# The forms of seven experts' W1 made while the routing runs, and new orders at both ends of the middle stage

## The chip, the cores and the metric

The kernel runs on one core of one Trainium2 chip. The metric is the time that one execution takes on the device, in microseconds (us); the kernel before was timed in three runs and the median counts. The engines are named as in the profile: PE is TensorE's matrix products and PEld its weight loads, DVE is VectorE, ACT is ScalarE, POOL is GpSimd, SP is SyncE. SPq and POOLq are the instructions by which an engine issues transfers (DMA). Each engine works through its own instructions in order, and a transfer is issued only when its engine has come to it.

## The reference

Attention with a polynomial sketch gives x: 4352 rows (4 batches of 1088) by 128 columns. Eight experts then work on every row, and a Sinkhorn normalization of the gate gives the weights P with which they are summed. All of it is float32.

```python
q_p, k_p = (phi(q), phi(k))                  # 64 sketch features per row
kv = np.einsum('bhsf,bhsd->bhfd', k_p, v)
z = np.sum(k_p, axis=2)
num = np.einsum('bhsf,bhfd->bhsd', q_p, kv)
den = np.einsum('bhsf,bhf->bhs', q_p, z)[..., None] + 1e-06
x = ...                                      # (4352, 128) from num / den
P = np.exp(logits - logits.max())            # logits = x @ w_gate, (4352, 8)
for _ in range(8):
    P /= P.sum(1, keepdims=True) + 1e-09
    P /= P.sum(0, keepdims=True) + 1e-09
    P *= N / E
for e in range(E):                           # w1[e]: 128 x 1024, w2[e]: 1024 x 128
    h = np.maximum(x @ w1[e], 0.0)
    out += P[:, e:e + 1] * (h @ w2[e])
```

## The kernel before

**Items and blocks.** The experts' work is cut into items: one expert with one group of columns of the transposed x (`xT`). An item has four blocks, each a quarter of the 1024 hidden units. Items that come early use x without the weights and keep their outputs (`kept`), which are weighted later; all others use x already multiplied by P. The expert products are computed by fast matrix products: sums of blocks of the operands are made first, so that fewer products are needed, and sums of the results afterwards. Which sums of W1 an item reads does not hang on x, so they can be made early: `forms_ahead` (line 256) makes two arrays in device memory for an expert, `wl` and `wf`. Expert 0 needs none, since all its items lie outside the middle stage.

**How the forms of one expert are made.** `forms_ahead(e, area)` returns nine jobs: `loads` (two copies of raw W1 into `wl`, three loads into the working area), `turn_all`, `turn_low`, `turn_lowest`, `turn_across` (four ScalarE instructions that copy with the sign turned, line 282; two of them also issue an addition), `keep_low`, `last_sum`, `keep_two`, `keep_rest`. Additions are transfers issued by POOL that add to their target (line 276); copies and stores are transfers issued by SP (line 279). The working area is 3 x 512 elements on each of 128 partitions.

**Three stages.** First comes the attention of the four batches, then the routing; both are generators whose `yield n` calls `fill(n)`, which lets the plain stage of the experts' work take steps beside them. The plain stage is `steps()`: first products of 128 rows in line 1113, relus in line 1117, second products in line 1546. `passed[0]` counts its steps, and `aside` holds jobs by step number. In `routing()` the forms of experts 1 to 5 (`AHEAD = 5`) are put into `aside`, the first from 7 steps after the routing's start and each next one 6 steps later, with the nine jobs at 0, 5, 6, 7, 11, 12, 15, 16 and 20 steps. Their areas are the tile `kp` and the attention's buffers `phs` and `rb`, one for each of four experts in turn. The routing ends with four transfers from `qT` to `pT` (line 696), the weights by expert; weighted items read rows of `pT` into `px`.

**The list at the end of the plain stage.** `TAIL` (line 1560) holds what is done beside the last two plain items, by step: it weights the first item of the middle stage (`weigh_half`, `copy_half`, `join_halves`), loads its raw W2 (`raw_second`) and its W1 forms, and weights the two halves of the second item. `first_second_forms` loads `wf` in two halves into `y` tiles; `first_weights`, when it comes after it, then loads `wl` alone, and when it comes first, both `wl` into a `w1` tile and `wf` into a `w2` tile. `w1` and `w2` tiles are also those of the plain stage.

**The middle stage.** `middle()` writes out by hand the order of 68 blocks (34 items). Each job has a time, and jobs are issued in the order of their times; the times set nothing but this order. A block has 28 first products of 64 x 64 in line 1279 (seven forms for each of two pairs of tiles), evacuations of them by ACT (lines 1308, 1310, 1314) and DVE (line 1319), sums on DVE (`SUMS`, line 1181) and 40 second products in line 1546. The usual times repeat every `PERIOD`:

```python
at_ = own[n] if 0 <= n < len(own) and own[n] is not None else n * PERIOD + usual
```

For the first four blocks the times come from a table, `SEAM`. Beside the blocks stand the loads of later items: `first_weights` (`w<-wl`, `w<-wf`), `raw_second` (`ws<-in_moe_w_dram`), `fetch_weights` (`px<-pT`). An expert's W2 forms are made from raw W2 by DVE (line 238) and ACT (line 241) the first time it is used, and stored with `keep_second` (line 251). In the second item's start `SEAM` has its two copies on ACT and four joins on POOL (line 842, `x2a` and `x2b`). The forms of W1 of experts 6 and 7 are also made here, in a tile `forms`, with the same nine jobs as in the routing (`forms_beside`, line 1557), expert 6 from block 1 on and expert 7 from block 5 on.

**The end.** After the last block of the middle stage, three unweighted blocks (`EARLY = 3`) take their first products (`step_of_two`) while the last sums go on. A last group follows, and the rest of the outputs are stored.

## Time and profile before

| What | Value |
|---|---|
| Median of 3 runs | 895.38 us (895.25 to 897.02) |
| Profiled execution, its own time | 898.83 us |
| Span of its instructions | 897.0 us |
| Granted TensorE clock, mean | 0.997 |
| TensorE busy, 0 to 175 us (attention, routing) | 171.2 us |
| TensorE busy, 175 to 235 us (end of plain stage, head of middle stage) | 58.6 of 60 us |
| TensorE busy, 235 to 327 us | 85.6 of 92 us |
| TensorE busy, 327 to 816 us | 489.0 of 489 us |
| TensorE busy, 816 to 897 us | 75.5 of 81 us |
| Device memory read and written | 125.7 MB and 25.1 MB |

The span runs from the first instruction to the last. A row of the profile names a line of the kernel, an engine, an operation and the tiles as output<-inputs, with partitions x elements and the count; a bracket at the end says how long the engine stood idle ahead of it, and what it waited for. A row of the table by stage has the window, then its length, the busy time of PE, PEld, DVE, ACT and POOL with the number of instructions, the granted clock, the share of the DMA engines that was busy, and GB/s. In the chain of waits the first figure is the time at which a step begins and the second its length. A row of transfers has the count, the size of each and the time from issue to landing.

### The profile page before, as it was taken

Reading aid. Unit: us, or ns where it says so; the run is one execution under the profiler, and the core shown is the slowest. Engines: PE = TensorE matmul, PEld = TensorE weight load, DVE = VectorE, ACT = ScalarE, POOL = GpSimd, SP = SyncE. Lnnn points to the kernel's source line nnn. Section 1 sums busy time; section 2 is a strip of 40 time slices with the busy share of each in tenths; the row PEclk is TensorE's granted clock in tenths of the full one; section 3 lists DMA queues with packets and bytes.
Section 4 is the critical chain, followed back from the end, with each engine's and each line's share of the span. In section 5 each row is a group of like instructions: output and inputs, shape, how many; then the busy total and the mean of one; then the engine's idle time right before and its main releaser. Section 6 shows DMA issues by size and latency. Waiting matters only on the chain.

```text
span 897.0 us, 28696 instructions
## 1 busy us (share of the span) xinstructions
PE 880.0 (98%) x11790; PEld 640.2 (71%) x11790; DVE 792.7 (88%) x1628; ACT 572.1 (64%) x1312; POOL 176.5 (20%) x244
## 2 busy tenths in 40 slices
PE   8999999999998989999999999999999999999997
PEld 6777644454776768887778878888778777766665
DVE  7678788888999979999999999899998999997865
ACT  3455477668776647676676766766766766755543
POOL 3121123112222212212212211231122122200000
PEclk9999999999999999999999999999999999999999
DMA  9996359687899777976787676787668776764340
GB/s 253 300 269 229 106 105 223 151 205 197 215 269 260 177 231 207 249 219 164 209 234 199 176 221 158 226 223 213 194 158 226 213 223 179 213 190 89 90 112 13
DMA packets 97459, 174.67 MB, mean 195 GB/s; under 512 B 29216, under 2 KB 68976, under 8 KB 92480
## 3 DMA queue, kind: packets, MB, share of 16 engines
q1 hardware_dynamic: 74832, 139.67, 49.7%
q0 software_dynamic: 21264, 33.00, 21.3%
q8 instruction: 93, 1.52, 0.7%
q10 hardware_dynamic: 1232, 0.16, 0.1%
q14 instruction: 38, 0.31, 0.1%
HBM read 125.70 MB, written 25.08 MB: 168 GB/s over the span
## 4 chain that ended last, share of the span: by engine, by line
PE 92%; DMA 4%; DVE 2%; ACT 1%; issue 0%; SPq 0%; POOL 0%; DVEq 0%; ACTq 0%
PE s L1546 41%; PE a L1279 36%; PE a L1113 12%; DMA kx<-in_k_dram 1%; PE a L419 1%; DMA w<-wf 1%; PE a L534 1%; DMA forms<-in_moe_w_dram 1%; DMA v<-in_v_dram 1%; DMA w<-wl 1%; DVE hb L1132 0%; PE a L386 0%; ACT hb L1314 0%; PE a L498 0%; DVE hb L1181 0%
## 5 line engine op out<-in xcount | busy, mean ns | idle before, releaser
L1279 PE MATMUL a<-xe,w 64*64 64x384 f32 x2164 | 419.7, 485 | 0.0
L1546 PE MATMUL s<-hb,ws 64*64 64x256 f32 (+4 forms) x2962 | 382.7, 384 | 1.8 <-DVE hb L1132 0.9
L1546 PE MATMUL s<-hx,ws 64*64 64x256 f32 (+1 forms) x2894 | 353.1, 378 | 0.0
L1279 PE MATMUL a<-de,w 64*64 64x384 f32 x1600 | 305.9, 483 | 6.1 <-DMA w<-wf 3.9
L1546 PEld LDWEIGHTS s<-hb,ws 64*64 64x64 f32 (+1 forms) x2962 | 207.0, 133 | 72.9 <-issue 23.1
L1546 PEld LDWEIGHTS s<-hx,ws 64*64 64x64 f32 (+1 forms) x2894 | 201.3, 134 | 54.1 <-issue 7.9
L1181 DVE TENSOR_TENSOR hb<-hb 128x512 f32<-128x512 f32 (+1 forms) x340 | 187.7, 577 | 2.3 <-ACT hb L1314 2.1
L1279 PEld LDWEIGHTS a<-xe,w 64*64 64x64 f32 x2164 | 147.3, 133 | 18.3 <-ACT hx L1314 1.7
L1314 ACT ACTIVATE hx<-a 128x384 f32<-128x384 f32 x204 | 96.6, 492 | 61.8 <-PE a L1279 60.6
L1314 ACT ACTIVATE hb<-a 128x384 f32<-128x384 f32 x204 | 97.6, 492 | 57.6 <-PE a L1279 56.0
L1279 PEld LDWEIGHTS a<-de,w 64*64 64x64 f32 x1600 | 112.5, 133 | 26.5 <-issue 4.4
L1113 PE MATMUL a<-xT,w 128*64 128x256 f32 (+3 forms) x576 | 130.1, 454 | 0.0
L1181 DVE TENSOR_TENSOR hx<-hx 128x512 f32<-128x512 f32 (+1 forms) x204 | 118.3, 594 | 0.5 <-ACT a L1308 0.5
L842 POOL DMA_DIRECT2D de<-xe x68 | 56.2, 964 | 281.9 <-ACT de L835 188.4
L1117 ACT ACTIVATE hb<-a 128x256 f32<-128x256 f32 (+3 forms) x148 | 66.5, 453 | 62.6 <-PE a L1113 53.2
L1310 ACT ACTIVATE hb<-a 128x384 f32<-128x384 f32 x136 | 66.7, 490 | 35.4 <-PE a L1279 34.2
L1319 DVE TENSOR_TENSOR a<-a,hb 128x384 f32<-128x384 f32 x136 | 76.7, 564 | 13.8 <-PE a L1279 12.3
L1308 ACT COPY a<-a 128x384 f32<-128x384 f32 x136 | 63.0, 463 | 34.6 <-PE a L1279 33.9
L1132 DVE TENSOR_TENSOR hb<-hb 128x416 f32<-128x416 f32 (+7 forms) x90 | 60.7, 674 | 19.4 <-ACT hb L1117 15.4
L1113 PEld LDWEIGHTS a<-xT,w 128*64 128x64 f32 x576 | 55.1, 137 | 28.1 <-issue 15.6
L1546 PE MATMUL s<-hb,w 128*64 128x256 f32 (+3 forms) x280 | 69.8, 435 | 0.0
L842 POOL DMA_DIRECT2D de<-de x34 | 30.0, 883 | 144.1 <-DMA de<-xe 72.5
(220 smaller groups left out, 1017.4 us busy)
## 6 DMA issues: line engine op xcount, KB each, us to landing
ws<-ws SPq DMA_DIRECT2D x34, 1280.0 KB, 6.5
w<-wl SPq DMA_DIRECT2D x34, 512.0 KB, 7.5
w<-wf SPq DMA_DIRECT2D x33, 512.0 KB, 8.2
px<-pT SPq DMA_DIRECT2D x34, 384.0 KB, 9.0
w<-in_moe_w_dram SPq DMA_DIRECT2D x16, 512.0 KB, 4.7
de<-xe POOLq DMA_DIRECT2D x34, 192.0 KB, 3.1
de<-de POOLq DMA_DIRECT2D x34, 192.0 KB, 8.2
ws<-in_moe_w_dram SPq DMA_DIRECT2D x7, 512.0 KB, 9.0
```

Of the source, the lines that this page charges most:

```text
L419: nc.tensor.matmul(pv[64 * s:64 * (s + 1), i], kp[0:n, H * t + h].rearrange("p i j -> p (i j)"), vx[0:n, slots[h], t, :], start=(t == 0 an ...
L842: tc.keep_in_program_order(nc.gpsimd.dma_start(out=out, in_=x, accum_op=Alu.add))
L1113: nc.tensor.matmul(ph[sl], loaded_w[j][0][:, P * f + H2 * s:P * f + H2 * (s + 1)], sources[j][:, lo:hi], start=True, stop=True, tile_posit ...
L1117: last_relu[:] = [nc.scalar.activation(out=out, in_=ph, func=Act.Relu).ins.name]
L1132: nc.vector.tensor_tensor(out, a, b, op=Alu.subtract)
L1181: nc.vector.tensor_tensor(places(out), places(a), places(b), op=Alu.subtract if off else Alu.add)
L1279: nc.tensor.matmul(out[sl], w[r, c0 + H2 * s:c0 + H2 * (s + 1)], x[r], start=start, stop=stop, tile_position=(H2 * row, H2 * s), skip_grou ...
L1308: witness(k, p, 1, nc.scalar.copy(b, bx))
L1310: witness(k, p, 5, nc.scalar.activation(out=m5s[p], in_=b, func=Act.Copy, scale=1.0 if p else -1.0))
L1314: ins = nc.scalar.activation(out=out, in_=x, func=Act.Relu)
L1319: ins = nc.vector.tensor_tensor(by if what == 1 else raw(k, p, 1, 1), bb[p], m5s[p], op=Alu.add)
L1546: mm = nc.tensor.matmul(sums[g][i][H2 * s:H2 * (s + 1), n * place:n * (place + 1)], w, x, start=c == (2 if t == 3 and row is None else 1) ...
```

## The change

Five things are changed.

1. The forms of all seven experts that need them (1 to 7) are made ahead, from `forms_of_all`, which is called in the last batch's attention after its `times(b, 0)`. Expert 1 begins 2 steps after that call, expert 2 eight steps after it (`AHEAD = 8`), and each next one 6 steps later. The nine jobs and their offsets stay.
2. Each expert has a working area of three pieces of 512 elements of its own, taken from the attention's buffers (`k`, `phs`, `rb`, `v_slots`) and `kp`. `forms_beside` and the tile `forms` go.
3. The copies and joins of the second item's x go from the middle stage into `TAIL`, and the rest of `TAIL` is moved by a step or two. `first_weights` now comes at step 15, ahead of `first_second_forms` at 16.
4. `SEAM` has other times, so that the first four blocks are issued in another order.
5. A second table, `DRAIN`, gives times for the last two blocks of the middle stage, the evacuations of their sums, the weighting ahead, and the three unweighted blocks' steps (four relu steps each, `R`, and their sums, `T`).

The sums, products and sizes of the experts' work stay as they are. The diff, with the tables cut:

```diff
--- before.py
+++ after.py
@@ -269,8 +269,8 @@
         w = split(moe_w1[e])
         fast[e] = [dram.tile([P, F], F32, name=f"{n}{e}") for n in ("wl", "wf")]
         wl, wf = (split(t) for t in fast[e])
-        rows = area.rearrange("p (i k f) -> p i k f", i=3, k=2)
-        d, t3, z = rows[:, 0], rows[lower, 1], rows[:, 2]
+        d, t3, z = (x.rearrange("p (k f) -> p k f", k=2) for x in area)
+        t3 = t3[lower]
 
         def plus(out, x):
             tc.keep_in_program_order(nc.gpsimd.dma_start(out=out, in_=x, accum_op=Alu.add))
@@ -287,27 +287,25 @@
             copied(nc.sync, t3, w[lower, :, 1])
             copied(nc.sync, z[lower], w[upper, :, 1])
 
-        x = area.rearrange("p (i n) -> p i n", i=3)
-
         def turn_all():
-            turn(x[:, 0], x[:, 0])
-            plus(x[:, 0], w[:, :, 1])
+            turn(area[0], area[0])
+            plus(area[0], w[:, :, 1])
 
         def turn_low():
-            turn(x[lower, 1], x[lower, 1])
+            turn(area[1][lower], area[1][lower])
             plus(t3, w[upper, :, 1])
 
         def turn_lowest():
-            turn(x[lower, 2], x[lower, 2])
+            turn(area[2][lower], area[2][lower])
 
         def turn_across():
-            turn(x[upper, 2], x[lower, 0])
+            turn(area[2][upper], area[0][lower])
 
         def keep_low():
             copied(nc.sync, wf[lower, :, 0], d[lower])
 
         def last_sum():
-            plus(x[:, 0], x[:, 2])
+            plus(area[0], area[2])
 
         def keep_two():
             copied(nc.sync, wl[lower, :, 1], t3)
@@ -576,12 +574,30 @@
         lo, hi = chunks[c]
         nc.vector.transpose(out=lgp[:, lo // 32:hi // 32, :].rearrange("p a e -> p (a e)"), in_=pg)
 
+    def forms_of_all():
+
+        def pieces(t, n):
+            t = t.rearrange("p a b -> p (a b)") if len(t.shape) == 3 else t.rearrange("p a b c -> p (a b c)")
+            return [t[:, F // 2 * i:F // 2 * (i + 1)] for i in range(n)]
+
+        kx = pieces(ld.tile([P, SA, D], F32, tag="k", name="kx", bufs=1), 2)
+        ph0, ph1, r = (pieces(t, 4) for t in (*phs, rb))
+        v0, v1 = (pieces(t, 2) for t in v_slots)
+        kp = pieces(wk.tile([P, (NT + 1) * H, R, R], F32, tag="kp", name="kp", bufs=1), 4)
+        areas = [*kx, v0[0]], ph0[0:3], [ph0[3], v0[1], kp[0]], kp[1:4], r[0:3], ph1[0:3], [r[3], ph1[3], v1[0]]
+        for e, area in enumerate(areas, 1):
+            begin = passed[0] + (2 if e == 1 else AHEAD + 6 * (e - 2))
+            for at_, do in zip((0, 5, 6, 7, 11, 12, 15, 16, 20), forms_ahead(e, area)):
+                aside.setdefault(begin + at_, []).append(do)
+
...
         times(b, 0)
+        if not follows:
+            forms_of_all()
         yield 2.2 if b == 1 else 2
...
     def routing():
 
-        kp = wk.tile([P, (NT + 1) * H, R, R], F32, tag="kp", name="kp", bufs=1)
-        areas = [t.rearrange("p i n -> p (i n)")[:, 0:3 * F // 2] for t in (*phs, rb)]
-        areas.insert(0, kp.rearrange("p a i j -> p (a i j)")[:, 0:3 * F // 2])
-        for i, e in enumerate(range(1, 1 + AHEAD)):
-            for at_, do in zip((0, 5, 6, 7, 11, 12, 15, 16, 20), forms_ahead(e, areas[i % 4])):
-                aside.setdefault(passed[0] + 7 + 6 * i + at_, []).append(do)
         yield 5
         for c in range(len(chunks)):
             logits(c)
...
-        SEAM = {"x2a": (0.199,), "x2b": (1.073,), "E2": (2.951,), "E3": (3.623,), "L1": (5.253,), "L2": (8.499,),
-                "L3": (10.157,), "F0_0": (9.663,), "F0_1": (4.383,), "F0_2": (4.405,), "F1_0": (0.91,),
...
+        SEAM = {"E2": (-0.166,), "E3": (1.446,), "L1": (3.286,), "L2": (6.411,), "L3": (6.474,), "F0_0": (7.042,),
+                "F0_1": (0.85,), "F0_2": (7.698,), "F1_0": (7.882,), "F1_1": (8.895,), "F1_2": (10.5,),
+                "F2_0": (0.248,), "F2_1": (-0.25,), "F2_2": (4.656,), "F3_0": (1.782,), "F3_1": (5.985,),
...
+        DRAIN = {"M1e": (-7.425, 0.993,), "M2e": (-4.759, 3.104,), "M3e": (-3.285, 5.419,), "M4e": (-2.23, 8.876,),
...
+                 "S1_9": (17.474, 27.21,), "w0": (1.221,), "w1": (7.77,), "w2": (8.37,), "w3": (15.452,),
+                 "w4": (17.621,), "E0": (21.824,), "E1": (27.288,), "E2": (27.523,), "E3": (27.542,), "A0": (23.79,),
+                 "A1": (26.516,), "A2": (26.761,), "R0_0": (18.654,), "R0_1": (18.18,), "R0_2": (18.225,),
+                 "R0_3": (17.814,), "T0_0": (20.881,), "T0_1": (22.709,), "R1_0": (23.329,), "R1_1": (24.792,),
+                 "R1_2": (23.849,), "R1_3": (23.916,), "T1_0": (26.989,), "T1_1": (27.09,), "R2_0": (29.259,),
...
+        end = len(ks) * PERIOD
+
+        def at_end(name, i=0):
+            return end - PERIOD + DRAIN[name][i]
 
         def when(name, n, usual):
+            if 0 <= n - len(ks) + 2 < 2 and len(DRAIN.get(name, ())) == 2:
+                return at_end(name, n - len(ks) + 2)
             own = SEAM.get(name, ())
             return own[n] if 0 <= n < len(own) and own[n] is not None else n * PERIOD + usual
 
@@ -1420,7 +1461,7 @@
         for n, k in enumerate([ks[0] - 1] + ks, -1):
             if k == ks[-1] or items[blocks[k][0]][0] != items[blocks[k + 1][0]][0]:
                 for i, at_ in enumerate(EMPTY):
-                    add(SEAM[f"C{i}"][0] if n < 0 else n * PERIOD + at_, evacuate, i)
+                    add(SEAM[f"C{i}"][0] if n < 0 else at_end(f"E{i}") if k == ks[-1] else n * PERIOD + at_, evacuate, i)
         for n, k in enumerate(ks):
             j, q = blocks[k]
             t = n * PERIOD
@@ -1444,8 +1485,8 @@
                         at_ = t + 3.9 + 2 * PERIOD * (i - j - 1)
                         add(at_, prepare_x, i)
                         add(at_ + 0.1, prepare_w, i)
-                    for i, at_ in enumerate((10, WEIGH, WEIGH + 0.3, PERIOD + 10, PERIOD + WEIGH)):
-                        add(t + at_, lambda: sums_ahead[j + 1].pop(0)())
+                    for i in range(5):
+                        add(at_end(f"w{i}"), lambda: sums_ahead[j + 1].pop(0)())
                 late = 2 if g == PLAIN else 0
                 if 1 + late <= es.index(e) <= es[0] + 1 + late:
                     weigh_kept(g, es.index(e) - 1 - late, t, add)
@@ -1474,7 +1515,7 @@
                 for i, at_ in enumerate(SECOND[row]):
                     add(when(f"S{row}_{i}", n, at_), second_product, k, i, row)
             for i, at_ in enumerate(EASE):
-                add(when(f"ls{i}", n + 1, at_), at_ease)
+                add(at_end(f"A{(0, 2, 1)[i]}") if k == ks[-1] else when(f"ls{i}", n + 1, at_), at_ease)
         fillers = [seven(k) for k in held_blocks]
         fillers = [ps for f in fillers for ps in f[:3]] + [fillers[i][3] + fillers[i + 1][3] for i in (0, 2)]
         for name, ps in zip(FILL, fillers):
@@ -1483,21 +1524,10 @@
             add(SEAM[name][0], evacuate, i)
         for i in range(1, 4):
             add(SEAM[f"L{i}"][0], at_ease)
-        for i in range(2):
-            add(SEAM["x2" + "ab"[i]][0], copy_half, first_new + 1, i)
-        add(SEAM["x2b"][0] + 1e-3, join_halves, first_new + 1)
         add(0.3, fetch_weights, first_new + 2)
         add(-0.3, make_second, first_new)
         for i, at_ in enumerate(FORMS_AT):
             add(at_, lambda i=i: forms_w2[first_new][i]())
-        t = 2 * PERIOD
-        for e, times in ((6, (10, 15.43, 20.13, t + 15.43, t + 20.13, t + 22, t + 24.5, t + 23.5, 2 * t + 14)),
-                         (7, (3 * t + 5, 3 * t + 15.43, 3 * t + 20.13, 4 * t + 6.6, 4 * t + 11.3, 4 * t + 12, 4 * t + 14.5,
-                              4 * t + 13.5, 5 * t + 6))):
-            own = []
-            add(times[0] - 0.1, lambda e=e, own=own: own.extend(forms_beside(e)))
-            for i, at_ in enumerate(times):
-                add(at_, lambda i=i, own=own: own[i]())
         add(SEAM["xm2"][0], weigh_half, first_new + 2, 0)
         add(SEAM["ac2"][0], copy_half, first_new + 2, 0)
         def begin_two(k):
@@ -1512,11 +1542,12 @@
         t = len(ks) * PERIOD
         for n in range(EARLY):
             k = ks[-1] + 1 + n
-            add(t + 4.6 * n + 3.4, begin_two, k)
-            for c in range(4):
-                add(t + 4.6 * n + 3.5, step_of_two, k, c)
-            for c in (4, 5) if n < EARLY - 1 else ():
-                add(t + 4.6 * n + 2.5 + 0.9 * c, lambda k, c: ready[k][2](c), k, c)
+            times = [at_end(f"R{n}_{c}") for c in range(4)]
+            add(min(times) - 1e-3, begin_two, k)
+            for c, at_ in enumerate(times):
+                add(at_, step_of_two, k, c)
+            for i in range(2) if n < EARLY - 1 else ():
+                add(at_end(f"T{n}_{i}"), lambda k, i: ready[k][2](4 + i), k, i)
         for _, _, do_ in sorted(jobs, key=lambda a: a[:2]):
             do_()
 
@@ -1552,15 +1583,15 @@
                 part(g, i)
         return mm
 
-    AHEAD = 5
-
-    def forms_beside(e):
-        return forms_ahead(e, pools[0].tile([P, 3 * F // 2], F32, name="forms", bufs=1))
-
-    TAIL = {12: ((weigh_half, first_new, 0), (raw_second, first_new, "ws4")), 13: ((copy_half, first_new, 0),),
-            14: ((weigh_half, first_new, 1), (first_second_forms, first_new)), 15: ((copy_half, first_new, 1),),
-            16: ((join_halves, first_new), (first_weights, first_new)), 18: ((weigh_half, first_new + 1, 0),),
-            20: ((weigh_half, first_new + 1, 1),), 21: ((evacuate, 0),), 23: ((evacuate, 1),)}
+    AHEAD = 8
+
+    TAIL = {12: ((weigh_half, first_new, 0), (raw_second, first_new, "ws4")),
+            13: ((copy_half, first_new, 0), (weigh_half, first_new, 1)), 14: ((copy_half, first_new, 1),),
+            15: ((join_halves, first_new), (first_weights, first_new)),
+            16: ((first_second_forms, first_new), (weigh_half, first_new + 1, 0)),
+            18: ((copy_half, first_new + 1, 0),), 20: ((weigh_half, first_new + 1, 1),),
+            21: ((evacuate, 0),), 22: ((copy_half, first_new + 1, 1), (join_halves, first_new + 1)),
+            23: ((evacuate, 1),)}
 
     def second(k, p):
         into(items[blocks[k][0]][0], *p)

```

90 rows, old and new, of tables (DRAIN, SEAM) are left out of this document.

## The prediction

> **What bounds the kernel now.** I read the page first, then TensorE's waits, the chain of waits in order of time, and the table by stage.
>
> ```profile
> span 897.0 us, 28696 instructions
> PE 880.0 (98%) x11790; PEld 640.2 (71%) x11790; DVE 792.7 (88%) x1628; ACT 572.1 (64%) x1312; POOL 176.5 (20%) x244
> ```
>
> TensorE (PE) is busy 98% of the span, and no matrix product is added or removed. So only time that TensorE loses can be won. Its two longest waits:
>
> ```profile
> PE a L1279 <- DMA w<-wf: 3.9, 1, 3.9
> PE a L1279 <- ACT a L1308: 2.2, 1, 2.2
> ```
>
> The chain gives the pitch. In the middle stage one block of L1279 and L1546 shows a run of 13 products once; from one start to the next is a block:
>
> ```profile
> 264.91 0.71 PE s L1546 x13
> 273.74 0.73 PE s L1546 x13
> 276.23 4.78 DMA w<-wl
> 281.53 5.82 DMA forms<-in_moe_w_dram
> ...
> 294.53 0.71 PE s L1546 x13
> ...
> 310.70 6.90 DMA w<-wf
> ...
> 327.15 0.74 PE s L1546 x13
> ...
> 724.80 0.72 PE s L1546 x13
> ```
>
> 273.74 - 264.91 = 8.83 us is the undisturbed pitch; the 45 blocks from 327.15 to 724.80 keep it (8.84 on the mean). From 273.74 to 294.53 are two blocks (17.66) and 3.13 us more; from 294.53 to 327.15 three blocks (26.49) and 6.13 us more. Sum lost: 9.26 us. The chain names the late work: the load of `forms` (W1 of expert 6 or 7, made beside the products) and the load of `wf` of expert 7. Of the 9.26, TensorE stood still 2.2 + 3.9 = 6.1 us; the rest is half-fed products and a slower clock (PEclk, the figure after the five engines):
>
> ```profile
> 287.00:290.00 3.00, 0.82 (x10) 0.36 (x12) 1.55 (x6) 2.57 (x7) 0.00 (x0) 1.00 0.54 120
> 318.00:320.00 2.00, 2.00 (x26) 1.64 (x22) 0.00 (x0) 0.97 (x3) 1.42 (x2) 0.73 1.02 435
> 320.00:325.00 5.00, 5.00 (x64) 3.77 (x60) 3.25 (x7) 2.77 (x7) 0.32 (x1) 0.76 0.93 233
> ```
>
> After the shorter stop the clock stays 1.00; after the longer it is 0.73 and 0.76: 0.27 x 2 + 0.24 x 5 = 1.7 us.
>
> **Part 1: forms of experts 6 and 7 leave the middle stage.** Away go, for each of the two, two copies of raw W1 into `wl`, three loads, four ScalarE turns, three GpSimd additions and four stores. They were issued beside the products on SP, ScalarE and GpSimd. The second stall's source is visible on the sync queue (SP): expert 7's last store goes out just ahead of the loads that read it back.
>
> ```profile
> 308.15 0.53 SPq L279 DMA_DIRECT2D wf<-forms x1
> 310.70 0.32 SPq L770 DMA_DIRECT2D w<-wf x1
> ```
>
> The first stall's source is ScalarE, which stands in order behind a turn that waits for its load. With the forms in DRAM a hundred microseconds earlier, neither is late, and of the blocks after 327 none is. Gain: 9.26, at least the 6.1 of standing still. Taken: -9.3. Next in line are the vector sums; VectorE is 88% busy over the span and keeps the pitch elsewhere.
>
> **Part 2: seven experts instead of five during the routing.** The distance of six steps (of the plain stage's schedule) between experts stays. Expert 1 began 7 steps after the routing's start; it now begins 2 steps after the start of the last batch's attention, which lies about 9 steps earlier (7.6 units at 0.87 per step): 14 steps ahead. Experts 2 to 7 follow from step 8 on, so expert 7 begins at step 38, where expert 5 began at 16 + 24 = 40. On SP the order is unchanged: forms of the last expert, then a load of W1, then `pT`.
>
> ```profile
> 100.19 2.19 POOL L560 DMA_DIRECT2D xT<-xd  x4 [3.38 <-DMA xd<-xt]
> 106.85 0.52 ACT L1117 ACTIVATE hb<-a 128x416 f32<-128x416 f32 x1 [0.18 <-PE a L1113]
> 119.21 0.62 ACT L282 ACTIVATE kp<-kp 128x512 f32<-128x512 f32 x1
> 120.14 2.15 POOL L276 DMA_DIRECT2D kp<-in_moe_w_dram  x2 [17.75 <-ACT kp L282]
> 152.17 0.63 ACT L282 ACTIVATE kp<-kp 128x512 f32<-128x512 f32 x1
> 163.50 4.55 SPq L279 DMA_DIRECT2D wf<-kp  x2
> 173.77 0.33 SPq L696 DMA_DIRECT2D pT<-qT  x1
> ```
>
> Per expert (152.17 - 119.21) / 4 = 8.2 us, so two experts more take 16.4. What the chain gains is set by its first addition on GpSimd (POOL), issued at 120.1 now. In the changed order it stands behind the four `xT` copies, which end at 100.19 + 2.19 = 102.4: 17.7 us earlier, more than 16.4. So the last store still goes out by about 168, ahead of `pT` at 173.8, which itself waits for the routing's last transpose. The two more experts' turns (8 of 0.63) and additions (6 of about 1.1) fill the stretch before 119 in which neither engine has any of them now; ScalarE is 64% busy over the span. With that cover gone they would cost their own 12 us at most. One wait is new: ScalarE's turn for expert 1 that reads the first addition stands just before a relu near 106, and the addition (issued at 102.4) lands, like the copies ahead of it that the logits need, some 3 to 6 us later, by 108. ScalarE (ACT) is held some 2 us, and TensorE, which runs a few product tiles `a` ahead of the relus, takes up part of it. Bounds 0 and +2; taken +0.5, near the lower since nothing of the routing waits there.
>
> **Part 3: the head of the middle stage.** Gone are two ScalarE copies (0.5 us each) and four GpSimd joins of the second item: between 0 and -1.5, taken -0.5. But the list at the end of the plain stage now calls `first_weights` ahead of `first_second_forms`. The first item therefore takes its `wf` from a `w2` buffer instead of `y`, and SP waits for buffers it did not wait for:
>
> ```profile
> 192.51 0.81 PE L1546 MATMUL s<-hb,w 128*64 128x384 f32 x4
> 198.98 0.54 PE L1279 MATMUL a<-de,y 64*64 64x384 f32 x2
> 199.85 0.42 SPq L786 DMA_DIRECT2D ws<-in_moe_w_dram x1
> 212.01 0.38 PE L1546 MATMUL s<-hb,w 128*64 128x256 f32 x1
> 216.87 0.42 DVE L238 TENSOR_TENSOR ws<-ws 128x256 f32<-128x256 f32 x1
> 217.63 0.57 DVE L1319 TENSOR_TENSOR a<-a,hb 128x384 f32<-128x384 f32 x1 [0.34 <-ACT hb L1314]
> 221.22 0.55 DVE L1319 TENSOR_TENSOR hb<-a,hb 128x384 f32<-128x384 f32 x1
> 221.83 0.54 PE L1279 MATMUL a<-xe,y 64*64 64x384 f32 x2 [1.43 <-DVE hb L1319]
> ws<-in_moe_w_dram SPq DMA_DIRECT2D x3, 512.0 KB, 8.9
> w<-wf SPq DMA_DIRECT2D x2, 512.0 KB, 5.7
> ```
>
> First buffer: free when expert 1's last product is read (193.3), landing 5.7 later at 199.0, needed at 198.98: just in time. Second buffer: expert 2's `w2`, read by the filler products until 212.4. SP holds the next item's `wf` until then (landing about 218.5, needed about 218.9), and queued behind it is the raw W2 load that now goes out at 199.85. It leaves at 212.8 and lands 8.9 later, at 221.7. VectorE (DVE) reaches its first reader (L238) after the sum of 217.63, at 218.2, and stands 3.5 us. Behind it stand a sum of 0.6 and the L1319 that TensorE needs: it ends at 221.7 + 0.4 + 0.6 + 0.5 = 223.2 instead of 221.8, so TensorE restarts 1.5 later than now, with about 0.8 us of VectorE's small sums still owed. Taken +2.0. Bounds: -1.9 (no such stand, and the 1.43 goes too) and +4.5 (a landing 2 us later). The wasted `y` load costs 512 KB on queues that are idle there: nothing.
>
> **Part 4: the drain.** On ScalarE four relus of the first unweighted block stand ahead of the weighted blocks' last relu, and VectorE waits for that one:
>
> ```profile
> 817.54 1.68 ACT L1117 ACTIVATE hx<-a 128x256 f32<-128x256 f32 x4
> 819.66 1.90 DVE L1181 TENSOR_TENSOR hb<-hb 128x512 f32<-128x512 f32 x3 [2.06 <-ACT hb L1314]
> ```
>
> In the new order that relu stands ahead of the four. It saves at most VectorE's 2.06; at worst the moved steps leave TensorE's row halves unpaired for one block of four (+1). Taken -1.2, near the row.
>
> **Sum.** -9.3 + 0.5 - 0.5 + 2.0 - 1.2 = -8.5 on this execution's 898.83 us (span 897.0 and 1.83 around it): 890.3. The median of the runs is 895.38, 3.45 below it. If the profiled run's excess sits in the stalls that go, the new median is about 890; if it sits elsewhere, 886.9. I take the middle, 888.5. A difference under 0.2% (1.8 us) cannot be told from no change here.
>
> **The rivals.**
> 1. The raw W2 load lands in time: it needs 5.4 us instead of 8.9. Then Part 3 gives -0.5 to -1.9 instead of +1.5: 885. For it: only two other loads are in flight then. Against: all three landings seen are near 8.9. Chance 0.25.
> 2. The stand at the head of the middle stage grows and slows the clock. TensorE would stand from about 219.9 to 223.3, 3.4 us, between the 2.2 that left the clock at 1.00 and the 3.9 that brought 0.73: +1.7, and with a landing 2 us later 893. Chance 0.15. [...]
> 3. Slower than before: the chain of seven ends late. If expert 1's additions were held until 120.1 as now, the last store would leave 16.4 us later, at 184.4, and `pT`, queued behind it on SP and GpSimd, 10.6 us late; the first weighted products follow `pT` without slack: 888.5 + 10.6 = 899. It decides once the first addition is later than about 110. Against it: nothing on GpSimd's queue ahead of it ends after 102.4. Chance 0.06.
> 4. No change: the loads of `wl` and `wf` are late for another reason, such as the freeing of their buffers: 895. Against: no other block waits for them. Chance 0.04.
>
> **How the numbers follow.** Forecast 0.50 at 888.5, its own range 886.5 to 891. Rivals 1 and 2 lie on both sides at 885 and 893; 883.5 to 893.5 leaves out rivals 3 and 4 and the tails of the two, 0.2. Faster: 0.50 + 0.25 + 0.15 = 0.90; same 0.04; slower 0.06.
>
> **What would show it.** Right: no `forms` tile, no wait for `wf`, and the pitch of 8.83 unbroken from 230 to 800 us (Part 1); first SP load of `pT` still near 174 (Part 2); VectorE idle 2 to 4 us near 218 ahead of the first L238, released by the `ws` load (Part 3); no VectorE wait above 1 us near 820 (Part 4). Wrong: a new TensorE wait over 2 us before 195 us, or a pitch above 8.83 in the middle.

## The result

The changed kernel takes 888.38 us (median of 4 runs, 887.2 to 889.62) against 896.13 us (895.25 to 897.02) for the kernel before in the same comparison. The ratio is 0.9914 with a 95% interval of 0.9894 to 0.9933: 0.9% faster. A later comparison, with 11 runs of the kernel before (median 895.41) and 6 of the changed one (888.37), puts the gain at 7.0 us. The profiled execution took 887.2 us.

The page of the changed kernel begins as follows; TensorE (PE) lost 8.7 us of its span where it had lost 17.0.

```profile
span 885.4 us, 28702 instructions
PE 876.7 (99%) x11790; PEld 626.5 (71%) x11790; DVE 792.0 (89%) x1628; ACT 571.9 (65%) x1309; POOL 176.4 (20%) x244
```

TensorE's waits after the change, with line, what it waited for, us in total, times and the longest. The two waits of 3.9 and 2.2 us are gone, and so is the 1.4 us behind a VectorE sum at the head of the middle stage. What is left of waits lies in the attention and the routing, but for one of 0.2 us; of the 8.7 us, 4.9 lie behind 860 us, at the end.

```profile
PE a L108 <- POOL own L110: 1.0, 1, 1.0
PE s L1577 <- DVE hb L1142: 0.9, 2, 0.7
PE a L1123 <- DVE kT L575: 0.7, 1, 0.7
PE a L462 <- ACT kvz L432: 0.6, 1, 0.6
PE s L1577 <- DVE hx L1329: 0.2, 1, 0.2
PE a L1123 <- DVE cr L697: 0.2, 1, 0.2
```

To see where the time went, four landmarks cut the execution into stretches: the issue of the last four `xT` transfers (POOL), the first product of the middle stage, a run of nine first products deep in the steady part of that stage, and the first eight products of the last group. The profile after has the first two in the rows of POOL and of PE by time:

```profile
98.96 2.20 POOL L558 DMA_DIRECT2D xT<-xd  x4 [3.52 <-DMA xd<-xt]
199.17 0.86 PE L1289 MATMUL a<-xe,w 64*64 64x384 f32 x4
```

and the other two in the chain of waits:

```profile
721.52 0.85 PE a L1289 x9
859.40 0.86 PE a L1123 x8
```

The answering rows of the profile before (its `xT` row, at 100.19, stands in the prediction), first from PE by time, then from the chain:

```profile
198.85 0.54 PE L1279 MATMUL a<-xe,w 64*64 64x384 f32 x2
```

```profile
731.05 0.85 PE a L1279 x9
871.01 0.86 PE a L1113 x8
```

The kernel before was profiled twice more in the experiments below, and the changed one once. The stretches of all five, each the difference of two such rows:

| Stretch | Before, three profiles | After, two profiles |
|---|---|---|
| Start to the `xT` transfers | 100.19, 98.73, 99.03 | 98.96, 99.95 |
| A: to the first product of the middle stage | 98.66, 98.73, 98.64 | 100.21, 100.29 |
| B: to the nine products in the steady part | 532.20, 528.10, 528.62 | 522.35, 522.15 |
| C: to the last group | 139.96, 140.41, 140.29 | 137.88, 137.88 |
| D: to the end of the span | 25.99, 26.03, 26.02 | 26.00, 26.03 |

The first stretch varies by 1.0 to 1.5 us between profiles of the same kernel, and its values before and after overlap; of the change it holds expert 1's loads and its first three turns (the first at 87.80 us in the first profile after). A became 1.6 us longer. B became 5.8 to 10.0 us shorter, and here the profile that the prediction had lies 3.6 to 4.1 us above the other two. C became 2.1 to 2.5 us shorter, D did not change.

### The profile page after: what moved, and what is told of

Read it like the earlier page. It is cut to its first block, busy times and chain, and to the rows that moved or that the text cites. A ratio compares the mean times of both kernels' runs of the same rounds, so it can differ in the third digit from the quotient of the medians.

```text
span 885.4 us, 28702 instructions
## 1 busy us (share of the span) xinstructions
PE 876.7 (99%) x11790; PEld 626.5 (71%) x11790; DVE 792.0 (89%) x1628; ACT 571.9 (65%) x1309; POOL 176.4 (20%) x244
## 4 chain that ended last, share of the span: by engine, by line
PE 83%; DVE 8%; issue 4%; DMA 3%; ACT 1%; POOL 1%; DVEq 0%; SPq 0%; POOLq 0%; ACTq 0%
PE s L1577 36%; PE a L1289 35%; PE a L1123 8%; DVE hb L1142 1%; DVE hb L1191 1%; DMA v<-in_v_dram 1%; DMA xd<-xt 1%; DVE hx L1191 1%; DVE ws L238 1%; PE a L108 1%; DMA ws<-in_moe_w_dram 1%; DMA kx<-in_moe_w_dram 1%; PE a L417 1%; POOL xT L558 0%; DVE a L1329 0%
## 5 line engine op out<-in xcount | busy, mean ns | idle before, releaser
L1289 PE MATMUL a<-de,w 64*64 64x384 f32 x1632 | 315.4, 483 | 0.0
L1577 PEld LDWEIGHTS s<-hb,ws 64*64 64x64 f32 (+1 forms) x2962 | 201.6, 133 | 75.5 <-issue 25.9
L1577 PEld LDWEIGHTS s<-hx,ws 64*64 64x64 f32 (+1 forms) x2894 | 195.9, 133 | 56.6 <-issue 11.9
```

Of the source, the lines that this page charges most:

```text
L1289: nc.tensor.matmul(out[sl], w[r, c0 + H2 * s:c0 + H2 * (s + 1)], x[r], start=start, stop=stop, tile_position=(H2 * row, H2 * s), skip_grou ...
L1577: mm = nc.tensor.matmul(sums[g][i][H2 * s:H2 * (s + 1), n * place:n * (place + 1)], w, x, start=c == (2 if t == 3 and row is None else 1) ...
```

## The experiments

**The kernel before, profiled again.** No edit.

> The kernel before, unchanged, for a second profile. In the first one the two stalls between 264.9 and 327.2 us cost 9.3 us; by the timed runs the forms alone gain 4.8, so here the stalls should cost some 4 to 6 us, and the start of the middle stage may lie 1 to 3 us later than 198.9. If the stalls are the same in every run, they cost 9.3 again, and the first 199 us have to be longer in the kernels with seven forms by some 4 us.

> The kernel before, unchanged, for a third profile. The first stall (near 286, 3 to 4 us) is there again, as in both; the second (wait for wf near 316) was in one of two, so either is possible, and the time tells which: 892 to 896 without it, 896 to 900 with it. From the end of the last four xT transfers' start to the middle stage's first product 98.7 us again (98.66 and 98.73 in the two), against 100.2 to 101.8 in the kernels with seven forms: Part 2's cost is then 1.5 us or more, not 0.5.

They took 893.77 and 894.41 us. TensorE's waits in the second profile, and then in the third (two longest each):

```profile
PE a L1279 <- ACT a L1308: 2.0, 1, 2.0
PE a L1279 <- DVE hb L1319: 1.4, 1, 1.4
```

```profile
PE a L1279 <- ACT a L1308: 2.6, 1, 2.6
PE a L1279 <- DVE hb L1319: 1.4, 1, 1.4
```

The first stall is there in all three profiles, the wait for `wf` only in the first: it was in one of three executions, and that one took 4.4 to 5.1 us longer than the other two. The spread of the timed runs (892.6 to 899.7 us before, 887.2 to 890.7 after) fits that; which of them had the wait isn't known. The first stall is not the same in each profile either. By windows of time (length, busy time of the five engines, granted clock, DMA share, GB/s), at the end of the stop in the first profile:

```profile
288.00:290.00 2.00, 0.63 (x8) 0.36 (x12) 0.55 (x3) 1.94 (x6) 0.00 (x0) 1.00 0.64 155
290.00:291.00 1.00, 1.00 (x22) 0.67 (x18) 0.65 (x2) 1.00 (x4) 0.00 (x0) 1.00 0.96 224
```

and in the second:

```profile
288.00:290.00 2.00, 1.82 (x16) 0.99 (x20) 0.36 (x1) 1.70 (x5) 0.00 (x0) 0.61 0.92 235
290.00:291.00 1.00, 1.00 (x12) 0.67 (x9) 1.00 (x3) 0.52 (x2) 0.19 (x1) 0.50 1.11 425
291.00:292.00 1.00, 1.00 (x16) 0.66 (x12) 1.00 (x2) 0.27 (x1) 1.00 (x2) 0.58 1.05 434
292.00:293.00 1.00, 1.00 (x22) 0.74 (x17) 0.00 (x0) 0.44 (x2) 0.47 (x1) 1.00 1.22 379
```

After a stop of 2.2 us the clock stayed at 1.00 in the one; after a stop of 2.0 us it was 0.61, 0.50 and 0.58 up to 292 us in the other: 0.39 x 2 + 0.50 + 0.42 = 1.7 us more.

**The forms alone.** The changed kernel with the old `SEAM` and `TAIL`, the second item's copies and joins back in the middle stage, and without `DRAIN`:

```diff
-        SEAM = {"E2": (-0.166,), "E3": (1.446,), "L1": (3.286,), "L2": (6.411,), "L3": (6.474,), "F0_0": (7.042,),
...
+        SEAM = {"x2a": (0.199,), "x2b": (1.073,), "E2": (2.951,), "E3": (3.623,), "L1": (5.253,), "L2": (8.499,),
...
+        for i in range(2):
+            add(SEAM["x2" + "ab"[i]][0], copy_half, first_new + 1, i)
+        add(SEAM["x2b"][0] + 1e-3, join_halves, first_new + 1)
...
-            15: ((join_halves, first_new), (first_weights, first_new)),
-            16: ((first_second_forms, first_new), (weigh_half, first_new + 1, 0)),
...
+            14: ((weigh_half, first_new, 1), (first_second_forms, first_new)), 15: ((copy_half, first_new, 1),),
+            16: ((join_halves, first_new), (first_weights, first_new)), 18: ((weigh_half, first_new + 1, 0),),
```

> The forms of all seven experts are made while the routing runs, as in the changed kernel; the orders of the head and of the end are the old ones, with the second item's copies and joins in the middle stage. By the forecast (Parts 1 and 2 carry the gain): both stalls between 273 and 327 us are gone (9.3 us on a profiled execution like the one before), the pitch is 8.83 from 230 us on, the wf load goes into y, no wait of VectorE for the raw W2. By the two medians, 7.8 us gained in all, of which the end takes 2.1 and the head 0.6: 896.1 - 5.1 = 891. The rival is that the new orders carry the gain: then this kernel stays above 893.

890.57 us (889.28 to 891.39), ratio 0.9941 (0.9928 to 0.9954), 4.8 us faster than the kernel before in the same comparison. Stretch B is 522.88 us in its profile: 9.3 less than in the first profile of the kernel before, 5.2 and 5.7 less than in the other two. C is 139.98, unchanged. So the forms alone carry about two thirds of the gain. In B they gain 5 to 6 us against two of the three profiles and 9 against the third; A gives 2.0 us of it back (100.70 in this profile).

**The head added.** The changed kernel without `DRAIN`, so that the last two blocks and the unweighted ones keep their usual times:

```diff
-            if 0 <= n - len(ks) + 2 < 2 and len(DRAIN.get(name, ())) == 2:
-                return at_end(name, n - len(ks) + 2)
...
-            times = [at_end(f"R{n}_{c}") for c in range(4)]
+            add(t + 4.6 * n + 3.4, begin_two, k)
+            for c in range(4):
+                add(t + 4.6 * n + 3.5, step_of_two, k, c)
```

> As the changed kernel, with the old order at the end of the middle stage (no second table). By the forecast the end was worth 1.2, by the profile after about 2.1: 888.4 + 1.2 to 2.1 = 889.6 to 890.5, with VectorE's wait of about 2 us for the last relu back near 810 us. The head against the kernel with the forms alone: 0.6 faster by the two profiles, 1.5 slower by the forecast. If the end's order is worth nothing, 888.4.

890.66 us (889.04 to 891.98), ratio 0.9944 (0.9930 to 0.9959): the same time as with the forms alone, though its stretch B, 522.23, is 0.65 shorter. So the timed runs can't tell the new head from the old one (each ratio is uncertain by 1.2 to 1.3 us), and the 0.65 us in B is a difference of two single profiles; a cost of 1.5 us, as forecast, is not there in B. The end is worth 890.66 - 888.37 = 2.3 us (the second value is that of the next experiment); C falls from 139.90 to 137.88.

**The changed kernel again.** No edit.

> The changed kernel, unchanged: a second profile and the interval. If the raw W2 load lands reliably in time, it lands again some 5.5 us after its issue near 213, VectorE waits less than 1 us for it, and the time is 887 to 890. If its landing was lucky in the first profile, VectorE stands 2 to 4 us and TensorE loses 1 to 3 near 220.

888.37 us (887.31 to 890.69), ratio 0.9922 (0.9906 to 0.9938). The raw W2 load in its profile: VectorE's first reader waits 0.23 us here, 0.49 in the first profile. The row of the first profile's load in the chain of waits shows its landing, 5.5 us after the issue, where the forecast took 8.9:

```profile
213.13 5.51 DMA ws<-in_moe_w_dram
```

The reader's row in the first profile, then in this one:

```profile
218.66 0.42 DVE L238 TENSOR_TENSOR ws<-ws 128x256 f32<-128x256 f32 x1 [0.49 <-DMA ws<-in_moe_w_dram]
```

```profile
219.48 0.42 DVE L238 TENSOR_TENSOR ws<-ws 128x256 f32<-128x256 f32 x1 [0.23 <-DMA ws<-in_moe_w_dram]
```

**The raw W2 later.** Half of it is loaded a second time into the same place, in order behind the first load:

```diff
         tc.keep_in_program_order(nc.sync.dma_start(
             out=raw_w2[j], in_=moe_w2[items[j][1]].rearrange("(fo fi) d -> fi fo d", fi=P)))
+        if j == first_new + 1:
+            tc.keep_in_program_order(nc.sync.dma_start(
+                out=raw_w2[j][:, 0:FO // 2],
+                in_=moe_w2[items[j][1]].rearrange("(fo fi) d -> fi fo d", fi=P)[:, 0:FO // 2]))
```

> The changed kernel, with half of the raw W2 of the second item loaded a second time into the same place right behind the first load, so that it lands some 4 us later, near 222.5 instead of 218.6 (the landing of 8.9 us that the forecast took gave 221.7). By Part 3's mechanism VectorE stands about 4 us ahead of its first reader and TensorE restarts 2 us or a little more later: 888.4 + 2.0 to 2.6 = 890.4 to 891.0. By rival 2 the stand also slows the clock: 893. If the order of the sums has slack there, 888.4.

891.51 us (889.61 to 892.76), 3.1 us slower than the changed kernel, ratio to the kernel before 0.9953 (0.9936 to 0.9969). The profile shows the whole of Part 3's mechanism, first VectorE's reader, which now stands as long as the forecast had it, then TensorE's row behind it, and the windows after it:

```profile
222.66 0.42 DVE L238 TENSOR_TENSOR ws<-ws 128x256 f32<-128x256 f32 x1 [3.31 <-DMA ws<-in_moe_w_dram]
```

```profile
224.21 0.68 PE L1293 MATMUL a<-xe,w 64*64 64x384 f32 x2 [2.22 <-DVE hb L1333]
```

```profile
224.00:226.00 2.00, 1.79 (x16) 1.54 (x20) 2.00 (x6) 0.42 (x2) 0.00 (x0) 0.62 1.13 396
226.00:228.00 2.00, 2.00 (x22) 1.32 (x18) 2.00 (x6) 0.77 (x3) 0.00 (x0) 0.53 0.85 196
```

TensorE stops for 2.2 us and then runs on a slower clock, 0.62 and 0.53, which costs 0.38 x 2 + 0.47 x 2 = 1.7 us. B is 726.13 - 200.34 = 525.8 us, 3.5 more than in the changed kernel. The median is 0.5 us above the forecast's price and below rival 2's 893; in this profile rival 2's mechanism is in it.

**One expert's forms beside the middle stage.** First expert 7's, at its old times and in the old tile:

```diff
-        for e, area in enumerate(areas, 1):
+        for e, area in enumerate(areas[:6], 1):
...
+        add(t + 4.9, lambda: own.extend(forms_beside(7)))
...
+            add(at_, lambda i=i: own[i]())
```

Then expert 6's, with expert 7 in its place in the routing:

```diff
-        for e, area in enumerate(areas, 1):
-            begin = passed[0] + (2 if e == 1 else AHEAD + 6 * (e - 2))
+        for e, area in zip((1, 2, 3, 4, 5, 7), areas):
+            begin = passed[0] + (2 if e == 1 else AHEAD + 6 * (min(e, 6) - 2))
...
+        add(9.9, lambda: own.extend(forms_beside(6)))
...
+            add(at_, lambda i=i: own[i]())
```

> The changed kernel, but the forms of expert 7 are made beside the middle stage again, at the times and in the tile that they had before (expert 6's stay in the routing). By Part 1 the wait for wf of expert 7 returns near 315, 6.1 of the 9.3 us in a profile like the first: 894.5; by the timed runs, in which both together were worth 4.8, two thirds of that: 891.6. If it was expert 6 alone that delayed the rest, 888.4.

> The changed kernel, but the forms of expert 6 are made beside the middle stage again, at the times and in the tile that they had before, and expert 7's take its turn in the routing. In the kernel with expert 7 beside, all of the 4.9 us was lost behind expert 7's turns and loads; no wait of TensorE in either profile of the kernel before lies behind expert 6's. So 888.4, and the pitch stays 8.83 from 230 us on. If the two stalls came from the load of the queues by either expert, 891 to 893, with a stall between 215 and 250.

With expert 7 beside: 893.32 us (891.55 to 897.28, 12 runs), ratio 0.9975 (0.9962 to 0.9989), 4.9 us slower than the changed kernel. TensorE's wait, and the ScalarE instruction ahead of it, which stands for its addition:

```profile
PE a L1289 <- ACT a L1318: 1.9, 1, 1.9
```

```profile
286.84 0.63 ACT L282 ACTIVATE forms<-forms 64x512 f32<-64x512 f32 x1 [2.96 <-DMA forms<-in_moe_w_dram]
```

With expert 6 beside: 889.93 us (887.96 to 890.95), ratio 0.9939 (0.9924 to 0.9954), and no stall; the longest wait that TensorE has between 200 and 330 us is 0.3 us:

```profile
PE a L1289 <- ACT hb L1324: 0.3, 1, 0.3
```

So the first stall belongs to expert 7's turn on ScalarE, as Part 1 has it. What the turn waits for is an addition, which GpSimd issues at 280.46 us here and at 281.53 in the first profile of the kernel before; Part 1 calls it a load. The runs up to 897.3 us suggest that the second stall comes and goes here too; the one profile shows the first alone. Expert 6 costs 0.7 us in B (522.96) and 1.6 by the medians, with intervals that overlap. (The medians of the experiments come from three comparisons, whose medians of the kernel before are 895.41, 895.59 and 894.74 us; differences of less than 1 us between comparisons mean little.)

**The forms later.** First where the five began before, 7 steps after the routing's start (`forms_of_all` is called at the head of `routing`); then 6 steps later than in the changed kernel:

```diff
-            begin = passed[0] + (2 if e == 1 else AHEAD + 6 * (e - 2))
+            begin = passed[0] + 7 + 6 * (e - 1)
+            begin = passed[0] + 6 + (2 if e == 1 else AHEAD + 6 * (e - 2))
```

> The changed kernel, but the seven experts' forms begin 7 steps after the routing's start, where the five began before, so the chain ends two experts (16.4 us) later than in the kernel before. By rival 3's price pT, or the work put ahead of it, is 10 us late: 899. Jobs that are still waiting when the routing ends are issued all at once there, and ScalarE then stands behind loads and additions: between 893 and 903. If the chain has that much slack, 888.4, and its early start was not needed.

> The changed kernel with all forms begun 6 steps later, so that expert 1's additions do not follow the xT transfers at once and its turns fall after 110; the chain ends some 8 us later, near 174.5, when pT goes out. If Part 2's cost of 1.5 to 3.1 us comes from ScalarE's turns ahead of the relus near 106, the stretch from the xT transfers to the middle stage's first product falls back to about 99 us and the time to 887. If the load of seven chains costs it, nothing changes: 888.4. If the last stores hold up px on SP, as with the forms 16 us late, it is slower: 890 to 892.

At the old place: 897.73 us (894.28 to 903.01), ratio 1.0028 (1.0009 to 1.0048), slower than the kernel before. Its sync queue, VectorE and TensorE:

```profile
186.35 0.53 SPq L279 DMA_DIRECT2D wf<-rb  x1
189.59 0.82 SPq L807 DMA_DIRECT2D px<-pT  x2
```

```profile
193.50 0.56 DVE L837 TENSOR_TENSOR xe<-xT,px 128x384 f32<-128x384 f32 x1 [6.89 <-DMA px<-pT]
```

```profile
194.58 0.90 PE L1576 MATMUL s<-hb,ws 128*64 128x384 f32 x1 [4.94 <-DVE hb L1141]
```

The last store goes out at 186.35 instead of 166.35, and the loads of `px` stand behind it on SP: 189.59 instead of 177.91. `pT` itself went out only 1 us later. VectorE waits for `px` with the plain stage's sums behind it, and TensorE waits for those. This is rival 3, with `px` in the place of `pT`.

Six steps later: 887.12 us (886.55 to 887.37), ratio 0.9909 (0.9895 to 0.9923), the fastest of all and the one with the narrowest spread. POOL's, PE's and SP's rows:

```profile
100.07 2.19 POOL L558 DMA_DIRECT2D xT<-xd  x4 [3.48 <-DMA xd<-xt]
```

```profile
199.31 0.86 PE L1289 MATMUL a<-xe,w 64*64 64x384 f32 x4
```

```profile
176.54 0.53 SPq L279 DMA_DIRECT2D wf<-rb  x1
180.76 0.82 SPq L808 DMA_DIRECT2D px<-pT  x2
```

Stretch A is 99.24 us, 1.0 less than in the changed kernel, and B (522.3) is the same. `px` goes out 2.9 us later, and VectorE waits 2.50 us for it at 186.83; TensorE has no wait between 175 and 199 us. Against the changed kernel it gains 1.2 us by the medians and 0.6 by what each gains on the kernel before in its own comparison; the intervals of the two ratios overlap, so that A's fall in the profile is the better evidence.

The rows tell where A fell. The routing's first exponential stands on VectorE's row behind a sum, and that sum waits for a relu of ScalarE. The sum's row in the changed kernel, then six steps later, then in the first profile before:

```profile
114.26 1.03 DVE L1142 TENSOR_TENSOR hb<-hb 128x832 f32<-128x832 f32 x1 [2.13 <-ACT hb L1127]
114.36 1.02 DVE L1142 TENSOR_TENSOR hb<-hb 128x832 f32<-128x832 f32 x1 [2.37 <-ACT hb L1127]
114.57 1.03 DVE L1132 TENSOR_TENSOR hb<-hb 128x832 f32<-128x832 f32 x1 [2.37 <-ACT hb L1117]
```

Counted from the `xT` transfers it begins after 15.30, 14.29 and 14.38 us, and the exponential after 19.1, 18.1 and 18.2. Between 105 us and that relu stand four of ScalarE's turns of 0.63 us in the changed kernel, three with the forms six steps later, none before. The products that make the logits begin after 7.10, 7.17 and 7.25 us: the transfers did not hold them up. So 0.9 of the 1.6 us is ScalarE's row. The other 0.6 lies between the exponential and `pT` (56.0 us against 55.4), is there with the forms six steps later too, and was not located.

**The list's order, and one turn.** First `first_second_forms` ahead of `first_weights` again, so that the first item's `wf` goes into `y`; then, on top of it, expert 1's `turn_across` three steps later:

```diff
-            15: ((join_halves, first_new), (first_weights, first_new)),
-            16: ((first_second_forms, first_new), (weigh_half, first_new + 1, 0)),
+            15: ((join_halves, first_new), (first_second_forms, first_new)),
+            16: ((first_weights, first_new), (weigh_half, first_new + 1, 0)),
...
-            for at_, do in zip((0, 5, 6, 7, 11, 12, 15, 16, 20), forms_ahead(e, area)):
+            for at_, do in zip((0, 5, 6, 7, 14 if e == 1 else 11, 12, 15, 16, 20), forms_ahead(e, area)):
```

> The changed kernel with first_second_forms ahead of first_weights in the list at the end of the plain stage, so that the first item's wf goes into y, as before. By Part 3: SP no longer waits until 212.4 for a w2 buffer, the raw W2 goes out near 200 and VectorE does not wait for it (0.5 us in the profile after). TensorE lost nothing there in the profile after, so 888.4, within 0.5. The rival is that VectorE's order passes every delay on, as the chain of waits after suggests: 0.5 faster.

> The changed kernel with wf in y (888.1), and expert 1's turn across, which waits up to 1.0 us for the first addition ahead of a relu near 106, issued 3 steps later. If that wait is Part 2's cost, the stretch from the xT transfers to the middle stage's first product falls from 100.3 towards 99.3 and the time to 887.2. If the turns' own work or the transfers cost it, 888.1.

888.06 us (887.69 to 889.29) and 888.42 us (887.51 to 890.23), ratios 0.9917 (0.9904 to 0.9929) and 0.9927 (0.9911 to 0.9943): neither can be told from the changed kernel. The first shows that the load order, which leads to a wasted load and to SP's wait until 212.8, costs nothing as long as the raw W2 lands in time. The second leaves A at 199.43 - 99.11 = 100.32 us: the one wait for the addition is not what Part 2 costs. In its profile four turns still stand between 105 us and the relu named above, the moved one last, at 113.84.

## Why the prediction came out right, and where its steps did not

The time lies within 0.2 us of the 888.5 that was predicted, and the sign and the range held. That it came so near is luck: Part 1 was too large by 3.8 us for a typical run, of which the middle between the two medians took back 1.6, and Part 2 too small by 1.1, while Parts 3 and 4 were worth 2.2 and 1.1 us more than forecast, and these errors cancel.

- **What bounds the kernel** was read rightly: most of the gain lies in time that TensorE lost in B. After the change the pitch is 8.84 us on the mean from 288.54 to 341.60 (six blocks) and from there to the run at 721.52 (43 blocks). It is not unbroken from 230 us on, as the prediction's sign has it: the five blocks from 242.74 to 288.54 take 9.16 us each. The chain's rows after:

```profile
242.74 0.85 PE a L1289 x9
288.54 0.85 PE a L1289 x9
341.60 0.85 PE a L1289 x9
```

- **Part 1**, -9.3: right to 0.1 for the execution that was profiled (532.20 against 522.88 with the forms alone). As a forecast of the typical run it was too large, as far as three profiles show, since the second stall is in one of them; the other two lose 5.2 and 5.7 us there. The step about the 3.45 us by which the profiled run exceeded the median named this ("If the profiled run's excess sits in the stalls that go, the new median is about 890"). That branch was the true one for this part, and the middle between the two branches had no reason of its own.
- **Part 2**, +0.5: the term was too small. A rose by 1.6 us in the changed kernel, and by 2.0 and 3.2 in the two kernels with parts of it; 3.2 lies outside the bound of 2. The named wait of ScalarE's turn was there but short (0.65 us, and none in the second profile), and issuing that turn later changed nothing. Beginning all forms 6 steps later took 1.0 of the 1.6 us back. The step that failed is "nothing of the routing waits there": the routing's first exponential does wait, behind VectorE's sum and the relu that ScalarE's four turns delay, which costs 0.9 of the 1.6 us by the rows shown with that experiment. No run takes the turns away and leaves the transfers, so that this is read from the rows; the other 0.6 stays open. The chain's end was forecast well: the last store went out at 166.35 (about 168 was said).
- **Part 3**, +1.5 in all: the failed step is the landing of the raw W2. It took 5.5 us in the first profile and 5.3 in the second, where 8.9 was taken from a row of three loads. That row rests on two landings, 8.7 and 9.2 us (the third has none in the trace), and not on three, as rival 1 says. A later load of the same profile, issued at 277.68, landed after 6.6 us, which spoke for rival 1 and was overlooked. SP did go out at 213.1 as worked out (212.8), and VectorE did wait, 0.2 to 0.5 us instead of 3.5. B fell by 0.65. So rival 1's condition is what happened; its 885 did not, because Parts 1 and 2 were too favourable.
- **Part 4**, -1.2: right in its mechanism, too small in size. VectorE's wait near 820 fell from 2.06 to 0.66 us (the row below), and C fell by 2.0 to 2.5 us, 2.3 in the timed runs. TensorE stood still for 0.6 us in C before and not at all after; the other 1.4 to 1.9 us went from time in which it counts as busy, and which order of the table won them was not tried. The sign "no VectorE wait above 1 us near 820" failed in its words: a new wait of 2.11 us for an unweighted block's relu stands at 817.70 us, and TensorE does not stop behind it.

```profile
809.14 1.90 DVE L1191 TENSOR_TENSOR hb<-hb 128x512 f32<-128x512 f32 x3 [0.66 <-ACT hb L1324]
```

- **Rival 2** was priced from a reading that doesn't carry over. A stop of 2.2 us was said to leave the clock at 1.00, from one row; in the windows after stops of 2.0, 2.6 and 2.2 us in the later profiles it fell to 0.50, 0.50 and 0.53 (the last section has these cases; what orders them was not shown). Had the raw W2 landed as late as the forecast took, the time would have been near 891.5, not 888.5, by the experiment that makes it late.
- **Rival 3** was right in kind and price: 899 was said, 897.7 measured, with `px` as the transfer that is late. Its point lies later than thought: with the last store at 176.5 us VectorE waits for `px` and TensorE does not; with it at 186.4 both wait.

A typical run's sum with the measured terms: B by the forms alone -5.5, A +1.6, the head -0.65, C -2.3: -6.9, against -7.0 measured in the longer comparisons.

## What to carry to other kernels

A stall that the profile shows once may be absent from most runs: when the profiled execution is slower than the median by about the size of a stall, subtract the stall, and profile a second time before pricing its removal. Work that is moved off a critical stage into a hidden one still has a price there, and its starting point can be tuned from both ends: here the forms of W1 cost 1.6 us when begun at once, 0.6 when begun 6 steps later, and 9 us more than at once when their last stores stood ahead of the next stage's loads on one queue. A stop of TensorE should be priced with the slower clock that may follow it: of the four stops of 2.0 to 2.6 us whose windows are given here, three were followed by one, at 1.7 us each. A median over a few rows should be read together with the rows: here the one short landing was in the profile.

## What the runs showed of the hardware

After the stop of 2.2 us in the first profile before, the granted clock stayed at 1.00 (288 to 291 us). After the stop of 2.0 us in the second it was 0.61 from 288 to 290 us, then 0.50 and 0.58 for 1 us each; after the stop of 2.6 us in the third 0.86 from 288 to 290 us, then 0.50, 0.50 and 0.57 for 1 us each; and after the stop of 2.2 us with the raw W2 late 0.62 and 0.53 for 2 us each. By these windows each of the three lost 1.7 us to the clock. The profile with the stop of 1.9 us (expert 7 beside) has a mean granted clock of 0.998 over its span, the same as with the raw W2 late, and the one with the forms late, where TensorE stood for 4.9 us, 0.995; both profiles of the changed kernel have 0.999. The stops' lengths don't order these cases, and what does was not shown.

Loads of raw W2, 512 KB each, landed between 6.6 and 9.9 us after their issue in the first profile of the kernel before (six landings), and between 5.3 and 9.4 in the two of the changed one, where the one at the head took 5.5 and 5.3. What sets it was not isolated.
